# Attention features: the exponential's bias on GpSimd, the last two normalisations on VectorE

## The chip, the cores and the metric

The kernel runs on one core of a Trainium2 chip. A core has five engines, each with its own in-order queue of instructions: TensorE (PE, with the weight loads shown apart as PEld), VectorE (DVE), ScalarE (ACT), GpSimd (POOL) and SyncE (SP), which here only issues DMAs. They wait for each other through semaphores. The metric is the device time of one execution in microseconds; three runs of the kernel before gave 2180.44 (the median), 2174.37 and 2181.72.

## The reference, cut to what matters

Three layers follow each other. The first is linear attention with random features on 4 batches of 8 heads, 576 rows of 64 each; then comes a mixture of 8 experts whose gate is balanced by eight rounds of scaling; then a layer of width 2048. The change is in the first one:

```
def phi(x):
    proj = np.einsum('bhsd,md->bhsm', x, omega)
    sq = np.sum(x * x, axis=-1, keepdims=True) / 2.0
    h = proj - sq
    h = h - np.max(h, axis=-1, keepdims=True)
    return np.exp(h) / np.sqrt(m)
q_p, k_p = (phi(q_s), phi(k_s))
kv = np.einsum('bhsm,bhsd->bhmd', k_p, v)
z = np.sum(k_p, axis=2)
num = np.einsum('bhsm,bhmd->bhsd', q_p, kv)
den = np.einsum('bhsm,bhm->bhs', q_p, z)[..., None] + 1e-06
return (num / den)
```

## The kernel before

Attention is cut into 16 units (4 batches of 4 pairs of heads) and each unit into five chunks of rows, 128 and four times 112. A loop (L548) runs 20 iterations of five rounds r = 0 to 4. In iteration i, round r computes the features of chunk r of unit i, and a written plan (PLAN, L541) adds the later steps of the units before: `qkT` (transposes of the next unit's q and k), `kv` and `zT` (sums over the keys of unit i-1), `qpT` (transposes of unit i-2's normalised query features) and `num` (the numerator of unit i-3). The order of the work is this loop's order; no scheduler changes it.

The features of one chunk (`feat`, L387) go through a chain of engines. TensorE writes the projections of q and k for two heads, `pr`, into one PSUM bank (L393). VectorE takes the maximum over the features, `mx` (L403), and makes the bias of the exponential in two small subtractions on 4 numbers a row: `nm` = squares minus maximum (L405) and `nb` = `nm` minus squares (L407). ScalarE then runs four exponentials (L412), which write `ek` and `eq`; they are issued first in the next round. The bank of `pr` is free once these four are done.

The 7 rotating PSUM banks are shared by `pr`, the transposes `tr` and `qt`, `kv` and the numerator `nd`. In the steady loop the transpose `qt` of round 3 takes the bank that `pr` of round 1 had, `pr` of round 3 the one of round 0, and `nd` of round 4 the one of round 2; so the built program lets each of them wait for the exponentials of that chunk.

GpSimd does four kinds of work in this loop. It squares q and k of the next unit (`tmp`, L357, one of 128x640 elements in each of the rounds 0 and 1), it scales their sums (`sq`, L361, 128x10, in rounds 2 and 4), it multiplies `eq` of unit i-2 by the reciprocal of the denominators (L478: three products of 256 columns in round 0, two in round 1), and once in an iteration, from the sixth on, it takes a step of the weights' preparation. The denominators come from VectorE: per chunk and head a product with a sum (`jk`, L465), ten in an iteration, and a reciprocal (L475) after the first six and after the last four.

The main loop takes these in the order: `tmp` before the round's flush; then `mx`; then, as the flush works off its list, the sums with their products; and after the first of the list's items the generator steps on to `nm`, then to `nb`. The last two units' sums stand in iterations 16 and 17, where no features are left.

Of the kernel before, what the change touches and what calls it, by code (L numbers as in the profile page):

```python
# [13 lines left out]
ALU = mybir.AluOpType  # L14
# [5 lines left out]
def performer_moe_kernel(ctx, tc, q, k, v, omega, wg, w1, w2, win64, wout64, out):  # L20
    nc = tc.nc
    B, H, S, D = q.shape
    M = omega.shape[0]
# [233 lines left out]
    with ExitStack() as actx, tc.manual_schedule():  # L257
        pp = actx.enter_context(tc.tile_pool(name="pp", bufs=7, space=PSUM))

        def bank(name):  # L260
            return pp.tile([P, 512], F32, tag="b", name=name)
# [10 lines left out]
        NUN = B * NP  # L272
# [114 lines left out]
        def feat(u, c):  # L387

            qk, sq = T["qk", u], T["sq", u]
            o, n = CH[c]  # L390
            ps = bank(f"pr{u}_{c}")
            for i in range(2):
                nc.tensor.matmul(  # L393
                    ps[:n, 2 * M * i : 2 * M * (i + 1)], qk[:, i, o : o + n], bd, start=True, stop=True
                )
            mx = a2.tile([P, 4], F32, tag="mx", name=f"mx{u}_{c}", bufs=4)
            nm = a2.tile([P, 4], F32, tag="nm", name=f"nm{u}_{c}", bufs=4)
            nb = a2.tile([P, 4], F32, tag="nb", name=f"nb{u}_{c}", bufs=4)
            ps4 = ps.rearrange("p (i m) -> p i m", i=4)
            eq = a2.tile([P, 2, M], F32, tag="eq", name=f"eq{u}_{c}", bufs=16)  # L400
            ek = a2.tile([P, 2, M], F32, tag="ek", name=f"ek{u}_{c}", bufs=7)
            T["eq", u, c], T["ek", u, c] = eq, ek
            nc.vector.tensor_reduce(mx[:n], ps4[:n], AX.X, ALU.max)  # L403
            yield
            nc.vector.tensor_tensor(nm[:n], sq[:n, c], mx[:n], ALU.subtract)  # L405
            yield
            nc.vector.tensor_tensor(nb[:n], nm[:n], sq[:n, c], ALU.subtract)  # L407

            def exps():
                for i in (2, 3, 0, 1):  # L410
                    dst = (eq, ek)[i // 2][:n, i % 2]
                    nc.scalar.activation(dst, ps4[:n, i], AF.Exp, bias=nb[:n, i : i + 1])  # L412

            later.insert(0, exps)
            yield
# [34 lines left out]
        def zT(u):  # L450

            ps = pp.tile([P, 512], F32, tag="z", name=f"z{u}", bufs=1)
            zr = T.pop(("zr", u))
            for h in range(2):
                nc.tensor.transpose(
                    ps[:, h * M : (h + 1) * M], zr[:, h].rearrange("p t d -> p (t d)"), ident
                )
            dn = den[u % 2]

            def sums(cs):  # L460
                for c in cs:
                    n = CH[c][1]
                    for h in range(2):
                        junk = a2.tile([P, M], F32, tag="junk", name=f"jk{u}_{c}_{h}", bufs=2)
                        nc.vector.tensor_tensor_reduce(  # L465
                            junk[:n],
                            T["eq", u, c][:n, h],
                            ps[:n, h * M : (h + 1) * M],
                            1.0,
                            1e-6,  # L470
                            ALU.mult,
                            ALU.add,
                            dn[:n, c, h],
                        )
                nc.vector.reciprocal(dn[:, cs[0] : cs[-1] + 1], dn[:, cs[0] : cs[-1] + 1])  # L475
                for c in cs:
                    eq, n = T["eq", u, c], CH[c][1]
                    nc.gpsimd.tensor_tensor(eq[:n], eq[:n], dn[:n, c].to_broadcast([n, 2, M]), ALU.mult)  # L478

            def first():  # L480
                sums([0, 1, 2])
                laterv.append((2, lambda: sums([3, 4])))

            laterv.append((2, first))
# [63 lines left out]
        for i in range(NUN + 4):  # L548
            for r, items in enumerate(PLAN):
                if r in NORM and i + 1 < NUN:  # L550
                    norms(i + 1, NORM.index(r))
                if r in RED and T.get("red"):
                    laterv.append((3, T["red"].pop(0)))
                flush(feat(i, r) if i < NUN else iter(()))
                for fn, off, arg in items:
                    if 0 <= i + off < NUN:
                        fn(i + off, *(() if arg is None else (arg,)))
                if r == 0:
                    load(i + 2, 0, 1)
                if r == 3:  # L560
                    load(i + 2, 2)
                if i > 4 and r == SPL:
                    next(wprep, None)
                if i > 2 * NP + 4 and r in (1, 3):
                    next(xprep, None)
# [462 lines left out]
```

## Time and profile before

| What | Value |
|---|---|
| Median of three runs | 2180.44 us |
| The profiled execution | 2176.08 us |
| Its span, first to last instruction | 2174.3 us |
| PE, PEld, DVE busy | 98%, 87%, 84% of the span |
| ACT, POOL busy | 48%, 64% |
| Mean granted TensorE clock | 0.994 of full |

Busy shares are of the whole span, and the attention stage is only its first 212 us. Matmuls are pipelined and their ends modelled, so 98% of PE is not PE at its peak. In a timeline a row is one instruction or a merged run of equal ones: its start, its length, the engine, the line, what it writes and reads, and in brackets how long its engine sat idle before it and what the profile takes for the cause. Where an instruction waits for several semaphores, the cause named can be one that had long been done.

### The profile page before, as it was taken

To read this page: it belongs to the slowest core of one execution; us is meant where nothing else is said; L and a number is where in the kernel's file an instruction comes from. 1 tells how busy PE (TensorE), PEld (TensorE's weight loads), DVE (VectorE), ACT (ScalarE), POOL (GpSimd) and SP (SyncE) were. 2 spreads that over 40 slices of the span, in tenths; PEclk is the share of its full clock that TensorE was granted. 3 is DMA by queue.
4 is the path that set the end of the run, shared out by engine and by line. 5 is a ranking of instruction groups with operands and counts; after the bars stand their busy time and mean duration, and the time that the engine had idled before them with its cause. 6 is when DMAs were issued, how large, how long until landed. Compare 5 with 4: busy or idle time off the path is not lost.

```text
span 2174.3 us, 33292 instructions
## 1 busy us (share of the span) xinstructions
PE 2126.5 (98%) x10800; PEld 1891.3 (87%) x10800; DVE 1834.6 (84%) x3459; ACT 1048.6 (48%) x2577; POOL 1398.6 (64%) x1631
## 2 busy tenths in 40 slices
PE   8998999999999999999999999999999999999998
PEld 6786689989899899899999899899999989989997
DVE  8887588889898788798889778788886689999997
ACT  6676333333333433333333443333333377878775
POOL 5554677676767767676766767676766535656654
PEclk9999999999999999999999999999999999999999
DMA  4442413222323222232322233332222231222221
GB/s 114 130 105 87 146 68 121 78 96 83 97 81 100 91 95 88 95 100 80 103 82 91 74 107 99 102 99 82 97 79 80 69 102 44 88 88 73 73 76 37
DMA packets 184382, 195.71 MB, mean 90 GB/s; under 512 B 53392, under 2 KB 142992, under 8 KB 184208
## 3 DMA queue, kind: packets, MB, share of 16 engines
q1 hardware_dynamic: 177200, 184.09, 26.6%
q10 hardware_dynamic: 7008, 9.51, 1.2%
q8 instruction: 85, 1.39, 0.3%
q14 instruction: 89, 0.73, 0.1%
HBM read 171.00 MB, written 22.54 MB: 89 GB/s over the span
## 4 chain that ended last, share of the span: by engine, by line
PE 68%; DVE 14%; issue 4%; ACT 4%; DMA 1%; POOL 0%; DVEq 0%; SPq 0%; ACTq 0%; POOLq 0%
PE l L836 35%; PE b L727 13%; PE e L727 9%; PE a L727 9%; DVE t L819 3%; DVE t L820 2%; DVE t L812 2%; DVE acc L860 2%; DVE v L83 1%; ACT v L82 1%; PE p L801 1%; ACT t L818 1%; DVE x L83 1%; ACT u L82 1%; DVE acc L858 1%
## 5 line engine op out<-in xcount | busy, mean ns | idle before, releaser
L836 PE MATMUL l<-v,h 128*128 128x512 f32 x4320 | 1052.4, 393 | 8.0 <-ACT h L824 3.7
L836 PEld LDWEIGHTS l<-v,h 128*128 128x128 f32 x4320 | 806.8, 188 | 167.4 <-ACT h L824 4.4
L83 POOL TENSOR_TENSOR v<-rs,v 128x512 fp32r<-128x512 f32 x216 | 290.7, 1350 | 331.2 <-PE l L836 179.4
L866 DVE SCALAR_TENSOR_TENSOR acc<-l,pt,acc 128x512 f32<-128x512 f32 x540 | 397.6, 744 | 123.1 <-PE l L836 119.3
L83 POOL TENSOR_TENSOR u<-s,u 128x256 fp32r<-128x256 f32 x384 | 298.3, 788 | 114.6 <-ACT u L82 88.2
L727 PE MATMUL b<-x,u 128*128 128x384 f32 x1728 | 351.9, 338 | 3.0 <-DVE t L762 2.2
L727 PEld LDWEIGHTS b<-x,u 128*128 128x128 f32 x1728 | 309.1, 188 | 19.3 <-DVE t L762 2.6
L82 ACT CAST u<-s 128x256 fp32r<-128x256 f32 x384 | 154.4, 405 | 260.3 <-POOL s L162 233.3
L83 POOL TENSOR_TENSOR u<-rq,u 128x256 fp32r<-128x256 f32 x288 | 227.9, 791 | 21.4 <-ACT u L82 20.2
L727 PE MATMUL a<-x,u 128*128 128x384 f32 x1152 | 233.7, 337 | 0.6 <-ACT xo L520 0.6
L727 PE MATMUL e<-x,u 128*128 128x384 f32 x1152 | 233.1, 337 | 0.0
L801 PE MATMUL p<-x,u 128*128 128x384 f32 x1152 | 214.2, 340 | 0.8 <-ACT u L82 0.7
L727 PEld LDWEIGHTS a<-x,u 128*128 128x128 f32 x1152 | 205.5, 188 | 9.0 <-ACT xo L520 1.0
L801 PEld LDWEIGHTS p<-x,u 128*128 128x128 f32 x1152 | 204.7, 190 | 6.4 <-POOL u L83 1.6
L727 PEld LDWEIGHTS e<-x,u 128*128 128x128 f32 x1152 | 203.9, 189 | 1.2 <-DVE h L741 0.6
L825 POOL TENSOR_TENSOR h<-t,h 128x384 fp32r<-128x384 f32 x96 | 105.2, 1096 | 153.0 <-ACT h L824 148.4
L738 ACT ACTIVATE h<-b 128x384 fp32r<-128x384 f32 x96 | 47.2, 491 | 256.1 <-DVE b L776 252.4
L82 ACT CAST v<-rs 128x512 fp32r<-128x512 f32 x240 | 146.7, 621 | 35.0 <-PE l L836 34.1
L738 ACT ACTIVATE h<-t 128x384 fp32r<-128x384 f32 x96 | 50.4, 525 | 231.7 <-DVE t L763 231.7
L82 ACT CAST u<-rq 128x256 fp32r<-128x256 f32 x288 | 117.3, 407 | 1.6 <-ACT xo L880 1.6
L83 POOL TENSOR_TENSOR u<-rqi,u 128x256 fp32r<-128x256 f32 x96 | 93.0, 989 | 38.9 <-ACT u L82 36.5
L750 ACT COPY t<-a 128x384 f32<-128x384 f32 x96 | 46.1, 480 | 101.8 <-PE a L727 99.5
(140 smaller groups left out, 3120.3 us busy)
## 6 DMA issues: line engine op xcount, KB each, us to landing
rq<-in_moe_w_dram SPq DMA_DIRECT2D x96, 512.0 KB, 3.8
rs<-in_moe_w_dram SPq DMA_DIRECT2D x192, 256.0 KB, 2.7
rqi<-win SPq DMA_DIRECT2D x24, 512.0 KB, 4.8
rs<-wout SPq DMA_DIRECT2D x48, 256.0 KB, 2.8
xt<-xd SPq DMA_DIRECT2D x24, 384.0 KB, 5.5
r<-in_moe_w_in_dram SPq DMA_DIRECT2D x32, 256.0 KB, 3.2
r<-in_moe_w_out_dram SPq DMA_DIRECT2D x32, 256.0 KB, 3.0
xd<-xo SPq DMA_DIRECT2D x32, 144.0 KB, 1.8
```

Source lines behind the costliest of these rows:

```text
L82: nc.scalar.copy(dst[:, 0], src)
L83: eng.tensor_tensor(dst[:, 1], src, dst[:, 0].bitcast(F32), ALU.subtract)
L727: nc.tensor.matmul(ps[:, :TB], u[:, wi, c], x[:, xi, c], start=(start and m == 0), stop=(stop and m == 5), skip_group_check=True,)
L738: nc.scalar.activation(h[:, 0], src, AF.Relu)
L750: nc.scalar.copy(s1, A)
L801: nc.tensor.matmul(ps, u1[f + i][:, wi, c], ux[state["x0"] + 2 * t + i][:, xi, c], start=(m == 0), stop=(m == 11))
L812: nc.vector.tensor_tensor(s, u, ps, ALU.mult)
L819: nc.vector.scalar_tensor_tensor(s, gb, B1, s, ALU.add, ALU.mult)
L820: nc.vector.scalar_tensor_tensor(s, ga, A1, s, ALU.add, ALU.mult)
L825: nc.gpsimd.tensor_tensor(lo, s, hi.bitcast(F32), ALU.subtract)
L836: nc.tensor.matmul(ps, hh[f][:, hi, t : t + P], u2[n + f][:, wi], start=(f == 0 and i == 0), stop=(f == len(hh) - 1 and i == 2),)
L866: V.scalar_tensor_tensor(a, ps, p[:, e : e + 1], a, ALU.mult, ALU.add)
```

## The change

`nm` and `nb` are issued on GpSimd instead of VectorE, for all 16 units and five chunks: 160 small instructions. The product of `eq` with the reciprocal is issued on VectorE for units 14 and 15 (`u >= NUN - 2`), ten instructions, and stays on GpSimd for the others.

```diff
-            nc.vector.tensor_tensor(nm[:n], sq[:n, c], mx[:n], ALU.subtract)
+            nc.gpsimd.tensor_tensor(nm[:n], sq[:n, c], mx[:n], ALU.subtract)
             yield
-            nc.vector.tensor_tensor(nb[:n], nm[:n], sq[:n, c], ALU.subtract)
+            nc.gpsimd.tensor_tensor(nb[:n], nm[:n], sq[:n, c], ALU.subtract)
...
                 for c in cs:
                     eq, n = T["eq", u, c], CH[c][1]
-                    nc.gpsimd.tensor_tensor(eq[:n], eq[:n], dn[:n, c].to_broadcast([n, 2, M]), ALU.mult)
+                    eng = nc.vector if u >= NUN - 2 else nc.gpsimd
+                    eng.tensor_tensor(eq[:n], eq[:n], dn[:n, c].to_broadcast([n, 2, M]), ALU.mult)
```

GpSimd's queue in rounds 0 and 1 of iteration 4 stood before as follows; a name holds the unit and, after it, the chunk (`eq2_3` is chunk 3 of unit 2):

```order
L357 TENSOR_TENSOR tmp5_0_760<-qn1_99 128x640
L478 TENSOR_TENSOR eq2_0_423<-eq2_0_423,den0_108 128x256
L478 TENSOR_TENSOR eq2_1_466<-eq2_1_466,den0_108 112x256
L478 TENSOR_TENSOR eq2_2_504<-eq2_2_504,den0_108 112x256
L357 TENSOR_TENSOR tmp5_1_809<-kn1_101 128x640
L478 TENSOR_TENSOR eq2_3_533<-eq2_3_533,den0_108 112x256
L478 TENSOR_TENSOR eq2_4_560<-eq2_4_560,den0_108 112x256
```

The same place of GpSimd's queue now:

```order
L357 TENSOR_TENSOR tmp5_0_760<-qn1_99 128x640
L479 TENSOR_TENSOR eq2_0_423<-eq2_0_423,den0_108 128x256
L479 TENSOR_TENSOR eq2_1_466<-eq2_1_466,den0_108 112x256
L479 TENSOR_TENSOR eq2_2_504<-eq2_2_504,den0_108 112x256
L405 TENSOR_TENSOR nm4_0_766<-sq4_580,mx4_0_765 128x4
L407 TENSOR_TENSOR nb4_0_767<-nm4_0_766,sq4_580 128x4
L357 TENSOR_TENSOR tmp5_1_809<-kn1_101 128x640
L479 TENSOR_TENSOR eq2_3_533<-eq2_3_533,den0_108 112x256
L479 TENSOR_TENSOR eq2_4_560<-eq2_4_560,den0_108 112x256
L405 TENSOR_TENSOR nm4_1_815<-sq4_580,mx4_1_814 112x4
L407 TENSOR_TENSOR nb4_1_816<-nm4_1_815,sq4_580 112x4
```

The bias of chunk 0 stands behind three products and that of chunk 1 behind all five and the second `tmp`; on VectorE each stood right behind the reciprocal that the products wait for.

VectorE's queue at the end of the last unit, in iteration 17, now:

```order
L475 RECIPROCAL den1_109<-den1_109 128x6
L479 TENSOR_TENSOR eq15_0_2813<-eq15_0_2813,den1_109 128x256
L479 TENSOR_TENSOR eq15_1_2851<-eq15_1_2851,den1_109 112x256
L479 TENSOR_TENSOR eq15_2_2884<-eq15_2_2884,den1_109 112x256
L465 ISA jk15_3_0_3065,den1_109<-eq15_3_2905,z15_3033 112x128
L465 ISA den1_109 112x1
```

Before, the sums of chunk 3 (`jk15_3_0`) followed the reciprocal at once and the three products ran on GpSimd; now they stand between the two.

## Rows read from the trace of the kernel before

**Rows 1.** Windows: busy time by engine (x instructions), clock, DMA share, GB/s.
```profile
0.00:212.00 212.00, 189.47 (x1127) 154.32 (x1128) 176.25 (x695) 143.40 (x463) 108.75 (x170) 0.98 0.41 106
```
**Rows 2.** Timeline of the weight loads, one steady iteration of attention.
```profile
117.48 0.41 PEld L345 LDWEIGHTS qt<-ident,eq 128*128 128x128 f32 x4 [0.70 <-POOL eq L478]
...
119.17 0.78 PEld L509 LDWEIGHTS nd<-qp,kz 128*128 128x128 f32 x4 [0.56 <-ACT eq L412]
...
129.13 0.41 PEld L345 LDWEIGHTS qt<-ident,eq 128*128 128x128 f32 x4 [0.70 <-POOL eq L478]
```
**Rows 3.** Timeline of ACT ahead of the second of these waits.
```profile
127.92 0.62 ACT L412 ACTIVATE ek<-pr,nb 112x128 f32<-112x128 f32 x2 [1.78 <-PE pr L393]
128.44 0.62 ACT L412 ACTIVATE eq<-pr,nb 112x128 f32<-112x128 f32 x2
128.94 0.57 ACT L376 ACTIVATE qk<-tr 128x464 f32<-128x464 f32 x1
```
**Rows 4.** Timeline of DVE, rounds 0 and 1 of the same iteration.
```profile
121.94 0.69 DVE L403 TENSOR_REDUCE mx<-pr 128x4 f32<-128x512 f32 x1 [1.11 <-PE pr L393]
...
123.91 0.19 DVE L475 RECIPROCAL den<-den 128x6 f32<-128x6 f32 x1
124.02 0.12 DVE L405 TENSOR_TENSOR nm<-sq,mx 128x4 f32<-128x4 f32 x1
...
125.97 1.29 DVE L405 TENSOR_TENSOR nm<-sq,mx 112x4 f32<-112x4 f32 x1
127.36 0.47 DVE L407 TENSOR_TENSOR nb<-nm,sq 112x4 f32<-112x4 f32 x1
```
**Rows 5.** Timeline of POOL over the same rounds.
```profile
124.25 1.78 POOL L478 TENSOR_TENSOR eq<-eq,den 128x256 f32<-128x256 f32 x3 [0.59 <-DVE nm L405]
126.00 1.25 POOL L357 TENSOR_TENSOR tmp<-kn 128x640 f32<-128x640 f32 x1
127.20 1.18 POOL L478 TENSOR_TENSOR eq<-eq,den 112x256 f32<-112x256 f32 x2
```
**Rows 6.** Timeline of POOL, a small instruction and what follows it.
```profile
85.31 0.24 POOL L361 TENSOR_SCALAR sq<-sq 128x10 f32<-128x10 f32 x1 [2.78 <-DVE nm L405]
85.63 0.73 POOL L164 TENSOR_TENSOR s<-rq 128x256 f32<-128x256 f32 x1
```
**Rows 7.** Timeline of POOL: round 0's products, first, an uneven, last two iterations.
```profile
29.19 1.21 POOL L478 TENSOR_TENSOR eq<-eq,den 128x256 f32<-128x256 f32 x2 [0.90 <-DVE nm L405]
...
78.10 1.75 POOL L478 TENSOR_TENSOR eq<-eq,den 128x256 f32<-128x256 f32 x3
...
172.54 1.75 POOL L478 TENSOR_TENSOR eq<-eq,den 128x256 f32<-128x256 f32 x3 [0.17 <-DVE nm L405]
...
185.00 1.78 POOL L478 TENSOR_TENSOR eq<-eq,den 128x256 f32<-128x256 f32 x3 [2.51 <-DVE nm L405]
```
**Rows 8.** Timeline of PE in the iteration of 78.10.
```profile
81.69 0.37 PE L345 MATMUL qt<-ident,eq 112*128 112x112 f32 x1 [1.47 <-POOL eq L478]
```
**Rows 9.** Windows behind that wait and in a late iteration with idle PE.
```profile
82.00:85.00 3.00, 3.00 (x8) 2.15 (x7) 2.18 (x8) 3.00 (x11) 0.45 (x2) 0.50 0.28 78
...
177.00:180.00 3.00, 1.60 (x9) 1.11 (x9) 2.90 (x11) 2.08 (x8) 0.68 (x2) 1.00 0.00 0
```
**Rows 10.** Timeline of several engines, iteration 15 and the end of unit 15.
```profile
187.67 0.63 ACT L412 ACTIVATE ek<-pr,nb 112x128 f32<-112x128 f32 x2 [1.04 <-PE pr L393]
...
201.40 0.19 DVE L475 RECIPROCAL den<-den 128x6 f32<-128x6 f32 x1
...
201.76 3.61 POOL L478 TENSOR_TENSOR eq<-eq,den 128x256 f32<-128x256 f32 x5 [2.94 <-DVE den L465]
...
202.44 0.18 DVE L475 RECIPROCAL den<-den 128x4 f32<-128x4 f32 x1
...
204.85 0.45 PE L345 MATMUL qt<-ident,eq 112*128 112x112 f32 x1 [0.26 <-POOL eq L478]
```
**Rows 11.** Lines of DVE in the attention stage: an elementwise product on SBUF.
```profile
L224 DVE TENSOR_TENSOR xt<-xt 128x768 f32<-128x768 f32 x3 | 2.9, 952 | 0.0
```

## The prediction

> **What bounds the kernel now.** I read the windows first, then the loop's timeline engine by engine, backwards from where TensorE waits. The attention stage is the first 212 us, and only it is touched; in it PE is busy 189 us, DVE 176, ACT 143 and POOL 109 [rows 1]. No engine is full by these shares, and POOL, which gets the work, has the most room; so the question is not who has time but which wait closes the loop.
>
> In the steady part one iteration repeats every 11.65 us: the transpose `qt` of round 3 starts at 117.48 and again at 129.13 [rows 2]. Both times PE has waited 0.70 us, and the row names POOL's product `eq`. That had ended: its last run starts at 127.20 and takes 1.18, so 128.38 [rows 5]. What ended last is on ACT: the exponentials of chunk 1 run from 127.92 to 128.44 + 0.62 = 129.06, and `qt` starts 0.07 us later [rows 3]. It takes the PSUM bank of that chunk's `pr`. The exponentials in turn had waited 1.78 us; the row names PE, but they start 0.09 us after `nb` of chunk 1 ended on DVE, at 127.36 + 0.47 = 127.83 [rows 3, 4]. So the loop is: `qt`, the matmuls behind it, `mx` of round 0, the six sums, the reciprocal at 123.91, the second half on DVE, `nb` of chunk 1, the exponentials, the bank, `qt`. DVE is on this path from 121.94, where it had waited 1.11 us for PE [rows 4], to 127.83. In the same way `nd` of round 4 waits 0.56 us for the exponentials of chunk 2 [rows 2].
>
> **What the change does to this loop.** On DVE `nm` and `nb` of chunk 1 stood right behind the second reciprocal. On POOL they stand behind three products, the pair of chunk 0, `tmp` and two products, in a queue that starts after the first reciprocal. Three terms:
>
> Taken away on DVE: `nm` of chunk 1 takes 1.29 us against 0.12 for that of chunk 0, and `nb` 0.47 [rows 4]. The long one runs beside POOL's `tmp`, 126.00 to 127.25 [rows 5]. Without it DVE would be through about 1.5 us earlier in each iteration.
>
> The Trainium skill ("SBUF — State Buffer", section "Who interferes with whom") says that a VectorE instruction with two SBUF inputs is blocked by a GpSimd instruction that reads SBUF until that one ends. The trace agrees: 1.29 us beside a `tmp` of 1.25. By that rule alone the change takes a blocked instruction away and the kernel gets faster; this is a rival below.
>
> Added on POOL: POOL can start the first product at 124.25, as before, since reciprocal, sums, `mx` and PE ahead of it are unchanged. By the start-to-start distances the three products take 126.00 - 124.25 = 1.75, `tmp` 1.20, the two products 1.18 [rows 5]: 128.38 without the new instructions. Two pairs come on top, of chunk 0 and of chunk 1. The trace has no such pair on POOL. The nearest row is the scaling of 128x10 elements, 0.24 us, with 0.32 to the start of the next instruction [rows 6]; so a pair costs 0.48 to 0.64, and I take 0.50. From below, 0.24 (each as short as on DVE, 0.12 [rows 4]); from above, 1.18 (each like a product of 256 columns, 1.78 / 3 = 0.59 [rows 5]). With 0.50, `nb` of chunk 1 ends at 128.38 + 1.00 = 129.38, against 127.83: **1.55 us later** (1.03 to 2.91). The exponentials, `qt` and all behind it come that much later, in each turn of the loop. Nothing hides it: DVE's gained time lies ahead of `mx`es that now wait for the same late PE, and ACT and PE only wait.
>
> `nb` of chunk 0 also moves, from behind the first reciprocal to about 126.5, 2 us later. The exponentials of chunk 0 then hold up `pr` of round 3, which takes their bank. That wait stands ahead of `qt` on PE's queue and shorter than the delay of `qt`; it is contained in the 1.55 and not added. In rounds 2 to 4 the pairs follow work that POOL has done early; the exponentials there are queued behind those of chunk 1 on ACT, so I cost these pairs at nothing, with at most 3 x 0.50 in an iteration if ACT were not the later one.
>
> How many turns: round 0's products begin with 29.19 and end with 185.00, 14 times [rows 7]. Thirteen of them, to 172.54, have the `tmp` of the next unit: 13 x 1.55 = 20.2 us. In the uneven one at 78.10, POOL is the late engine already (PE waits 1.47 us for a product there [rows 8]); its chain, 78.10 + 1.75 + 0.50 + 1.20 + 1.18 + 0.50 = 83.2, and 1.2 for exponentials, lets `qt` start at 84.5, where now its last part starts at 81.69: 3 us instead of 1.55, so 1.5 more. The one at 185.00 has no `tmp`: 185.00 + 1.75 + 0.50, then 1.18 + 0.50, makes 188.93, and the exponentials start at 187.67 now, so about 0.09 after a `nb` of 187.58 [rows 10]: 1.35. Iterations 0 and 1 have no products; POOL's `tmp` blocks the pair on either engine, so 0, with 1 us to either side.
>
> **The second edit.** For units 14 and 15 nothing competes for DVE. Unit 15's first reciprocal ends at 201.59, POOL's products then take 3.61 us, and the transpose of chunk 3 starts at 204.85 [rows 10]. A product on DVE I put at 0.39 us, an estimate between 0.952 for 768 columns [rows 11] and 0.12 for 4 [rows 4]. Then 201.59 + 3 x 0.39, the sums and reciprocal of the second half (202.62 - 201.59 = 1.03 [rows 10]) and one product give 204.18: 0.67 gained, for two units 1.3. Bounds: nothing (blocked by POOL's own splits in the same stretch) and 2.5.
>
> **The sum.** 20.2 + 1.5 + 1.35 - 1.3 = +21.8 us. On the profiled execution, 2176.08: 2197.8. That execution is 4.4 below the median shown; the mean of it and the three runs is 2178.2, and I predict from that: **2200.0 us**. The later stages are bound by their own work and move back as a whole.
>
> **Rivals.**
> 1. The lock was the cost (faster). If the pair on POOL finished as early as a DVE free of blocking would have, PE could win back its waits, 0.70 + 0.56 = 1.26 us an iteration [rows 2], 13 x 1.26 + 1.3 = 17.7: 2160.5. For it: the 1.29 us row. Against: POOL is in order, and the row of products is now ahead of the pair. It decides if the pair ends before 127.83.
> 2. The delay is swallowed (no change). ACT idles 1.78 us ahead of these exponentials [rows 3], and the other banks could carry PE on. Against: that idle time is the wait for `nb` itself, and the bank follows within 0.07 us. It would leave only the tail's -1.3: 2177.
> 3. The clock falls too (slower still). PE's waits grow from 1.26 to 2.8 us an iteration. After the wait of rows 8 the granted clock was 0.50, that is 1.2 GHz, for at least 3 us [rows 9], which costs half of that, 1.5. In every turn this is 13 x 1.5 = 19.5 more: 2219.5. Against: a late stretch with PE busy for 1.60 of 3 us kept 1.00 [rows 9], and the new waits are split over `pr`, `qt` and `nd`. The page "TensorE: Matmul & The Clock Gate" of the Trainium skill, section "Part 1: The HAM clock gate", ties the clock to recent idleness; the two windows agree as far as they go.
>
> **How the numbers follow.** Forecast 0.78, rival 1 0.06, rival 2 0.06, rival 3 0.10. The forecast's own range, with a pair from 0.24 to about 0.9 and the tail's bounds, is 2190 to 2213. The range for 8 in 10 is 2188 to 2215, which takes in a clock that falls in some turns. A change of 0.3% (6.5 us) is what can be told from none here: slower 0.88, the same 0.06, faster 0.06.
>
> **What would show it.** The starts of round 0's products are 13.2 us apart instead of 11.65. On POOL `nm` and `nb` take about 0.25 each, behind the products; ACT's exponentials of chunk 1 start some 5.2 us after the first product instead of 3.7; PE's waits ahead of `pr` of round 3 and `qt` together grow by 1.55; DVE shows no `nm` of over 1 us and idles instead. The first matmuls of the next stage begin some 21 us later. If the products' starts stay 11.65 apart, the loop is not closed by these exponentials and I am wrong; if they come 14.7 or more apart with a clock below 1.00, rival 3 holds.

## The result: slower, by 0.66%

The changed kernel took 2192.11 us (median of five, 2188.38 to 2198.97) against 2180.44 for the kernel before (five runs, 2174.37 to 2181.91). The medians are 11.7 us apart, 0.54%. The ratio estimated from the runs is 1.0066, with an interval from 1.0054 to 1.0079, which is 12 to 17 us. The profiled execution took 2192.11 us; its span is 2190.3, against 2174.3 before.

The change lies in the attention stage, which ends 19.7 us later: the first weight load of the next stage starts at 230.68 instead of 210.96 (timelines of the weight loads, before and after).

```profile
210.96 1.01 PEld L727 LDWEIGHTS a<-x,u 128*128 128x128 f32 x6 [1.04 <-ACT xo L520]
```
```profile
230.68 0.99 PEld L728 LDWEIGHTS a<-x,u 128*128 128x128 f32 x6 [1.04 <-ACT xo L521]
```

What DVE gave away is seen in the windows over the stage (in the order of [rows 1]): DVE is busy for 142 us instead of 176, POOL for 132 instead of 109. PE is busy for 195 us instead of 189, but of 231 us instead of 212: its busy share falls from 89% to 84%.

```profile
0.00:231.00 231.00, 194.84 (x1123) 158.17 (x1124) 141.85 (x545) 143.49 (x463) 131.69 (x320) 0.97 0.37 97
```

The timeline of POOL in a steady iteration, over the rounds of [rows 5]:

```profile
125.77 1.76 POOL L479 TENSOR_TENSOR eq<-eq,den 128x256 f32<-128x256 f32 x3 [0.70 <-DVE den L475]
127.48 0.20 POOL L405 TENSOR_TENSOR nm<-sq,mx 128x4 f32<-128x4 f32 x1
127.76 0.20 POOL L407 TENSOR_TENSOR nb<-nm,sq 128x4 f32<-128x4 f32 x1
127.91 1.25 POOL L357 TENSOR_TENSOR tmp<-kn 128x640 f32<-128x640 f32 x1
129.12 1.18 POOL L479 TENSOR_TENSOR eq<-eq,den 112x256 f32<-112x256 f32 x2
130.26 0.20 POOL L405 TENSOR_TENSOR nm<-sq,mx 112x4 f32<-112x4 f32 x1
130.54 0.20 POOL L407 TENSOR_TENSOR nb<-nm,sq 112x4 f32<-112x4 f32 x1
...
138.64 1.76 POOL L479 TENSOR_TENSOR eq<-eq,den 128x256 f32<-128x256 f32 x3 [0.70 <-DVE den L475]
```

The products start 138.64 - 125.77 = 12.87 us apart instead of 11.65. A pair takes 127.91 - 127.48 = 0.43 us. The bias of chunk 1 ends at 130.74, 4.97 us after the first product; before it was 127.83 - 124.25 = 3.58. The timelines of ACT and of the weight loads (compare [rows 3] and [rows 2]) show who waits for it:

```profile
127.99 0.62 ACT L412 ACTIVATE ek<-pr,nb 128x128 f32<-128x128 f32 x2 [3.02 <-POOL nb L407]
...
130.78 0.63 ACT L412 ACTIVATE ek<-pr,nb 112x128 f32<-112x128 f32 x2 [1.14 <-POOL nb L407]
131.29 0.63 ACT L412 ACTIVATE eq<-pr,nb 112x128 f32<-112x128 f32 x2
```
```profile
129.19 0.70 PEld L393 LDWEIGHTS pr<-bd,qk 128*112 128x112 f32 x4 [0.94 <-ACT eq L412]
...
131.99 0.41 PEld L345 LDWEIGHTS qt<-ident,eq 128*128 128x128 f32 x4 [1.17 <-POOL nm L405]
...
133.45 0.78 PEld L510 LDWEIGHTS nd<-qp,kz 128*128 128x128 f32 x4 [0.33 <-ACT eq L412]
```

`pr` of round 3 now waits for the exponentials of chunk 0, `qt` for those of chunk 1 (they end at 131.92, `qt` starts 0.07 later; the row names `nm`, which was done at 130.46), `nd` for those of chunk 2. Together 2.44 us an iteration against 0.70 + 0.56 = 1.26 [rows 2]: 1.18 more, which is nearly the whole growth of the period, 1.22. DVE has no long `nm` any more and idles instead:

```profile
127.18 0.68 DVE L403 TENSOR_REDUCE mx<-pr 112x4 f32<-112x512 f32 x1
...
130.35 0.69 DVE L403 TENSOR_REDUCE mx<-pr 112x4 f32<-112x512 f32 x1 [1.76 <-PE pr L393]
```

In the uneven iteration (weight loads, then windows) `pr` waits 4.88 us, and in the 5 us behind it the granted clock is 0.55 of full, close to the lower of its two levels, 1.2 GHz:

```profile
89.03 1.30 PEld L393 LDWEIGHTS pr<-bd,qk 128*112 128x112 f32 x4 [4.88 <-ACT eq L412]
```
```profile
90.00:95.00 5.00, 5.00 (x16) 3.79 (x15) 1.28 (x4) 4.38 (x16) 1.55 (x8) 0.55 0.07 25
```

### The profile page after: what moved, and what is told of

It is laid out like the page before. It is cut to its first block, busy times and chain, and to the rows that moved or that the text cites. A ratio compares the mean times of both kernels' runs of the same rounds, so it can differ in the third digit from the quotient of the medians.

```text
span 2190.3 us, 33353 instructions
## 1 busy us (share of the span) xinstructions
PE 2130.7 (97%) x10800; PEld 1895.5 (87%) x10800; DVE 1796.4 (82%) x3309; ACT 1050.2 (48%) x2577; POOL 1421.5 (65%) x1781
## 3 DMA queue, kind: packets, MB, share of 16 engines
q8 instruction: 85, 1.39, 0.3%
## 4 chain that ended last, share of the span: by engine, by line
PE 81%; DVE 8%; issue 4%; POOL 3%; ACT 2%; DMA 2%; SPq 0%; DVEq 0%; POOLq 0%; ACTq 0%
PE l L837 41%; PE b L728 13%; PE a L728 9%; PE e L728 9%; PE p L802 6%; PE pr L393 1%; DVE t L820 1%; POOL eq L479 1%; POOL tmp L357 1%; DVE t L821 1%; DMA qn<-in_q_dram 1%; DVE t L813 1%; DVE x L83 1%; PE nd L510 1%; DVE acc L861 1%
## 5 line engine op out<-in xcount | busy, mean ns | idle before, releaser
L403 DVE TENSOR_REDUCE mx<-pr 112x4 f32<-112x512 f32 (+1 forms) x80 | 54.6, 683 | 74.1 <-PE pr L393 73.5
```

## The experiments

Each ratio is against the kernel before, run on the same chip. "Period" is the distance between the starts of round 0's products in a steady turn. Where a stretch of a profile is compared, it is one profile of each kernel. The question is what made the loop longer: the two instructions as such, the engine that they are on, or their place in GpSimd's queue; and whether the second edit bought anything.

**Only the first edit** (all products on GpSimd):

```diff
-                    eng = nc.vector if u >= NUN - 2 else nc.gpsimd
+                    eng = nc.gpsimd
```

> All 80 bias pairs on GpSimd, the products of units 14 and 15 left on GpSimd as before. Theory (the place in GpSimd's queue closes the loop): round 0's products start 12.88 us apart as in the changed kernel, against 11.65 before; the end of unit 15 looks like the kernel before, so it ends 0.5 to 1.5 us later than the changed kernel: ratio to before 1.007 to 1.008. Rival (each small GpSimd instruction costs, wherever it stands): the same time, so this run tells only the second edit's share.

2192.66 us, ratio 1.0060 (1.0046 to 1.0074), period 12.87. So the first edit is the whole loss. But the stage did not end later than in the changed kernel, as was expected: the next one starts at 229.83, 0.85 earlier. The total does not tell what the second edit is worth; the parts tell more. From the last iteration's first product (204.26 here, 206.17 in the changed kernel) to that start it is 25.57 us here and 24.51 there: by these two profiles the second edit gains 1.06 us. The 1.9 that this run was ahead by then is the difference between two executions of the same loop.

**Only the second edit** (the bias back on VectorE):

> Only the second edit: products of units 14 and 15 on VectorE, the bias stays on VectorE. By the prediction's step the attention stage ends 1.3 us earlier than in the kernel before, so the next stage's first matmul at 209.7 us, ratio 0.9994. By the other theory, taken from the changed kernel's trace (the last product took 0.93 us beside GpSimd's split instead of 0.42) and from the run without this edit, whose stage ended 0.85 us earlier than the changed kernel's, it gains nothing: first matmul at 211.0 to 212.0, ratio 1.0000 to 1.0005. The place of that matmul decides, since the times cannot tell these apart.

The next stage starts here:

```profile
209.92 1.01 PEld L728 LDWEIGHTS a<-x,u 128*128 128x128 f32 x6 [0.99 <-ACT xo L521]
```

1.04 us earlier than before, 0.75 of it behind the last iteration's first product (25.21 against 25.96 us). This speaks against the theory of no gain, and the prediction's 1.3 looks a little too much; but both rest on single profiles, and the same stretch differs by more between kernels that all have this edit (23.47 to 26.79 us). The time was 2172.60, ratio 0.9982 (0.9973 to 0.9991): clearly faster, and by more than this gain. In the two profiles the rest is behind attention, where the kernels are alike: from that load to the end it is 2170.2 - 209.92 = 1960.3 here and 2174.3 - 210.96 = 1963.3 before.

**Only the pair of chunk 1 on GpSimd**, second edit kept:

```diff
-            nc.gpsimd.tensor_tensor(nm[:n], sq[:n, c], mx[:n], ALU.subtract)
+            be = nc.gpsimd if c == 1 else nc.vector
+            be.tensor_tensor(nm[:n], sq[:n, c], mx[:n], ALU.subtract)
...
-            nc.gpsimd.tensor_tensor(nb[:n], nm[:n], sq[:n, c], ALU.subtract)
+            be.tensor_tensor(nb[:n], nm[:n], sq[:n, c], ALU.subtract)
```

> Only the pair of chunk 1 on GpSimd, second edit kept. If the loop is closed by the bias of chunk 1 behind all five products and the second tmp, that bias ends at 128.38 + 0.44 = 128.82 instead of 127.83: 0.99 later, period 12.4 to 12.65 us, ratio 1.0045 to 1.006. If the cost is mostly that of chunk 0's pair, whose exponentials hold the bank of pr in round 3 (0.94 us of wait there in the changed kernel), the period stays at or below 11.9 and the ratio at or below 1.0015.

2186.16 us, ratio 1.0042 (1.0030 to 1.0054), period 12.25: between the two forecasts, nearer to the first. The timelines of POOL and of the weight loads say why:

```profile
121.34 1.78 POOL L480 TENSOR_TENSOR eq<-eq,den 128x256 f32<-128x256 f32 x3 [0.47 <-DVE nm L406]
...
125.72 0.20 POOL L408 TENSOR_TENSOR nb<-nm,sq 112x4 f32<-112x4 f32 x1
```
```profile
127.17 0.41 PEld L345 LDWEIGHTS qt<-ident,eq 128*128 128x128 f32 x4 [1.71 <-POOL sq L361]
...
128.34 0.89 PEld L511 LDWEIGHTS nd<-qp,kz 128*128 128x128 f32 x4
```

The bias ends 125.92 - 121.34 = 4.58 us after the first product, 1.00 later than before, as computed, and `qt` waits 1.01 longer. But `nd` no longer waits at all, where it had 0.56: a wait that grows takes over a part of the next one on the same queue. So 1.01 - 0.56 = 0.45 is what the two waits add; the period grew by 0.60, and where the other 0.15 lies was not found.

**The pairs of chunks 2 to 4 on GpSimd**, those of 0 and 1 on VectorE (`c > 1` in the same place):

> The changed kernel, but only the pairs of chunks 2, 3 and 4 on GpSimd; those of chunks 0 and 1 on VectorE as before. Theory: the pair of chunk 1 is again right behind the second reciprocal, so the period stays 11.65 us and the ratio is 0.999 to 1.001, although 48 of 80 pairs have moved. Rival (cost by the instruction): three fifths of the loss, 1.004.

2178.26 us, ratio 0.9999 (0.9990 to 1.0008). The verdict is the first theory's, the period is not: 12.08 instead of 11.65, because `nd` waits 0.98 for chunk 2, whose pair stands behind GpSimd's scaling of `sq`, and that waits for VectorE's sum (weight loads; POOL one turn later):

```profile
123.23 0.78 PEld L511 LDWEIGHTS nd<-qp,kz 128*128 128x128 f32 x4 [0.98 <-ACT eq L413]
```
```profile
133.30 0.24 POOL L361 TENSOR_SCALAR sq<-sq 128x10 f32<-128x10 f32 x1 [0.86 <-DVE sq L360]
133.61 0.20 POOL L406 TENSOR_TENSOR nm<-sq,mx 112x4 f32<-112x4 f32 x1
```

The prediction had cost these pairs at nothing; alone they cost 0.43 us a turn. The next stage starts at 216.62, 5.7 us later than before. The total shows nothing of it: in the two profiles 2.6 us are made up behind attention (see below), and the other 3.1 are not seen in the ratio.

**All pairs on GpSimd, but ahead of the products:**

```diff
             nc.gpsimd.tensor_tensor(nm[:n], sq[:n, c], mx[:n], ALU.subtract)
-            yield
             nc.gpsimd.tensor_tensor(nb[:n], nm[:n], sq[:n, c], ALU.subtract)
...
+            def prods(cs):
...
+                laterv.append((2.5, lambda: prods([3, 4])))
...
             laterv.append((2, first))
+            laterv.append((2.5, lambda: prods([0, 1, 2])))
```

> The changed kernel with the pair issued ahead of the products in GpSimd's queue, tmp still ahead of the pair. Theory: the pair of chunk 1 waits for three products and tmp, not for the two products behind it: it ends at 127.20 + 0.44 = 127.64 in the clock of the kernel before, 0.2 us ahead of 127.83; period about 11.45 us, ratio 0.997 to 1.000. Rival (cost by the instruction, 80 pairs on GpSimd): 1.0066 as the changed kernel.

2178.72 us, ratio 1.0001 (0.9991 to 1.0010), period 11.82. The number of instructions on GpSimd is that of the changed kernel, and of the 1.22 us that a turn had lost 1.05 are back: what cost was the place. The next stage starts at 214.97, still 4.0 us later than before; that the total shows no loss is due to the stretch behind attention, 4.2 us shorter in this profile. The pair of chunk 1, still behind the second `tmp`, ends where it was expected, 118.74 - 115.34 = 3.40 us after the first product. The gain did not come all the same: `qt` waits a little less, 0.57 instead of 0.70, but `nd` waits 0.85 instead of 0.56 for chunk 2, whose pair now stands behind the two products and the scaling of `sq` (POOL, then weight loads):

```profile
117.05 1.25 POOL L357 TENSOR_TENSOR tmp<-kn 128x640 f32<-128x640 f32 x1
118.26 0.20 POOL L405 TENSOR_TENSOR nm<-sq,mx 112x4 f32<-112x4 f32 x1
118.54 0.20 POOL L406 TENSOR_TENSOR nb<-nm,sq 112x4 f32<-112x4 f32 x1
118.69 1.18 POOL L480 TENSOR_TENSOR eq<-eq,den 112x256 f32<-112x256 f32 x2
```
```profile
119.98 0.41 PEld L345 LDWEIGHTS qt<-ident,eq 128*128 128x128 f32 x4 [0.57 <-POOL eq L480]
...
121.96 0.78 PEld L513 LDWEIGHTS nd<-qp,kz 128*128 128x128 f32 x4 [0.85 <-ACT eq L411]
```

**The same, with `tmp` issued behind the round's flush, in rounds 1 and 2:**

```diff
-        NORM, RED, SPL = (0, 1), (2, 4), 4
+        NORM, RED, SPL = (1, 2), (3, 4), 4
...
-                if r in NORM and i + 1 < NUN:
-                    norms(i + 1, NORM.index(r))
...
                 flush(feat(i, r) if i < NUN else iter(()))
+                if r in NORM and i + 1 < NUN:
+                    norms(i + 1, NORM.index(r))
```

> As the last one, and the squares of the next unit (tmp) issued after the products of round 1 and after the features of round 2, their sums in rounds 3 and 4. Theory: the pair of chunk 1 ends at 126.00 + 0.44 = 126.44, 1.4 us ahead of the kernel before; TensorE gets back its waits of 0.70 and 0.56 us, the period falls to 10.4 to 10.7 us, ratio 0.991 to 0.995. Rival (cost by the instruction): 1.0066. Second rival (TensorE has another wait right behind): period above 11.3, ratio 0.998 to 1.000.

2167.86 us, ratio 0.9947 (0.9932 to 0.9961), period 11.33: faster than both kernels. The ratio is the first theory's, the period that of the second rival, another wait right behind: `qt` has no wait left; `nd` has, since chunk 2's pair now stands behind the first `tmp` (1.25 us):

```profile
103.73 0.78 PEld L513 LDWEIGHTS nd<-qp,kz 128*128 128x128 f32 x4 [0.76 <-ACT eq L411]
```

**Both `tmp` in rounds 2 and 3** (`NORM = (2, 3)`):

> Like the variant with the bias before the products and tmp behind the flush, but with the two tmp in rounds 2 and 3 instead of 1 and 2, so that the pair of chunk 2 stands ahead of both. If the position in GpSimd's queue is the whole cost, the 0.76 us wait of nd goes too: period 10.4 to 10.8 us, ratio 0.990 to 0.993 against the kernel before. If the late tmp and its sum on VectorE become the late ones instead (the squares for the next unit are then ready only in round 4), the period stays at 11.2 or above and the ratio at 0.994 or above.

2170.78 us, ratio 0.9974 (0.9965 to 0.9983). The loop does what the first theory says, 10.7 us, but the ratio does not. Over three turns PE is busy all of the time at the full clock (windows):

```profile
101.17:133.40 32.23, 32.23 (x212) 28.46 (x212) 23.77 (x97) 26.43 (x89) 25.09 (x61) 1.00 0.44 111
```

But the first product starts at 33.69 us, where it was 28.33 with `tmp` in rounds 1 and 2: in the first iterations the exponentials come late (weight loads), and the gain is eaten at the start.

```profile
21.09 0.30 PEld L423 LDWEIGHTS kv<-vn,ek 112*128 112x128 f32 x2 [1.96 <-ACT ek L411]
```

**Only the later `tmp`**, bias and products as in the kernel before:

> The kernel before with only tmp moved behind the flush of rounds 2 and 3; both edits undone, the bias on VectorE. If the place of tmp was all that the kernel before lacked, nm of chunk 1 is no longer blocked for 1.29 us, the period falls to 10.4 to 10.8 us and the ratio to 0.990 to 0.993, as good as with the bias on GpSimd. If the pair on VectorE is then blocked by the products (0.59 us each) and that of chunk 2 by tmp, the period is 11.0 to 11.6 us and the ratio 0.996 to 1.000, and the move of the bias to GpSimd is worth something once it is placed ahead.

2188.48 us, ratio 1.0054 (1.0041 to 1.0066), period 12.56: slower than either theory allowed. The timelines of DVE and POOL:

```profile
117.18 2.41 DVE L407 TENSOR_TENSOR nb<-nm,sq 112x4 f32<-112x4 f32 x1
```
```profile
117.18 1.19 POOL L478 TENSOR_TENSOR eq<-eq,den 112x256 f32<-112x256 f32 x2 [0.17 <-DVE nm L405]
118.32 1.26 POOL L357 TENSOR_TENSOR tmp<-qn 128x640 f32<-128x640 f32 x1
```

`nb` of chunk 1 starts with the first of two products and ends at 119.59, when the `tmp` behind them ends (119.58). That is 4.36 us after round 0's first product (115.23), where it was 3.58 before. In both places of `tmp` that were tried, the bias on VectorE was stopped by what GpSimd did at that moment; on GpSimd it is only queued, and that can be arranged. So the move of the bias is worth something once it stands ahead. Whether the bias on VectorE, with the products put later as in the runs above, would do as well was not tried.

**The last version**: `tmp` in rounds 1 and 2 in the first two iterations and in 2 and 3 from then on:

```diff
-                if r in NORM and i + 1 < NUN:
-                    norms(i + 1, NORM.index(r))
+                at = NORM if i > 1 else (1, 2)
+                if r in at and i + 1 < NUN:
+                    norms(i + 1, at.index(r))
```

> The bias on GpSimd ahead of the products, the two tmp behind the flush of rounds 1 and 2 in iterations 0 and 1 and of rounds 2 and 3 from then on. With both in rounds 2 and 3 throughout, PE was busy without a gap at a period of 10.7 to 10.8 us, but round 0's products began at 33.69 instead of 28.33 us. If those 5.4 us were lost only because the first two iterations waited for the later squares, the first matmul of the next stage falls from 205.8 to 200.4 to 201.5 us, ratio 0.992 to 0.9945 against the kernel before. If the start is regained but lost again in the uneven iteration, where a load decides, it stays at 204 to 206 us and the ratio at 0.996 to 0.9975.

2164.87 us (2158.43 to 2168.52), ratio 0.9936 (0.9919 to 0.9953), the lowest of all, though the interval overlaps that of 0.9947. It contains the second edit, which alone gave 0.9982. The first theory holds: the next stage starts at 200.58, 9.3 us earlier than with the second edit alone, and in the middle of the stage PE is busy for 39.9 of 40 us (weight load; windows).

```profile
200.58 1.01 PEld L732 LDWEIGHTS a<-x,u 128*128 128x128 f32 x6 [0.99 <-ACT xo L524]
```
```profile
110.00:150.00 40.00, 39.90 (x260) 34.98 (x259) 30.30 (x121) 32.07 (x108) 30.40 (x73) 1.00 0.41 107
```

## Why the prediction was right, step by step

The median was put at 2200.0 us, and 2192.11 lies inside the range. The profiled execution was put at 2197.8 and took 2192.11: 5.7 less, 2.0 of it in the attention stage and 3.7 behind it. The other 2.1 is that the forecast for the median was counted from a mean that lay above the profiled execution. The mechanism was right: the loop is closed by the bias of chunk 1, and GpSimd's queue makes it later. Two runs show it: the pair of chunk 1 alone on GpSimd brings nearly two thirds of the loss (1.0042 of 1.0066), and the reordered kernel, with as many instructions on GpSimd, has a period of 11.82 us instead of 12.87. The sizes, from the starts of round 0's products in the two profiles (29.19 and 30.32 for the first, 185.00 and 206.17 for the last) and the start of the next stage:

| Term | Predicted | Measured |
|---|---|---|
| Bias of chunk 1 later, in a steady turn | 1.55 | 4.97 - 3.58 = 1.39 |
| Period, in a steady turn | 1.55 | 1.22 (11.65 to 12.87) |
| Iterations 0 and 1, to the first product | 0 +- 1 | 1.13 |
| From the first to the last product, 13 turns | 20.2 + 1.5 = 21.7 | 20.04 |
| From the last product to the next stage | 1.35 - 1.3 = 0.05 | 24.51 - 25.96 = -1.45 |
| Behind attention, to the end of the span | 0 | 1959.6 - 1963.3 = -3.7 |
| Sum, on the profiled execution | 21.8 | 16.0 |

The period was put 0.33 us too long. Of this 0.14 is the pair, 0.43 us where 0.50 was taken, twice. The other 0.19 is that only the delay of `qt` was counted: `nd`'s wait fell from 0.56 to 0.33, since `qt` now stands longer ahead of it. The run with chunk 1 alone shows the same exchange in full, 0.56 to nothing.

The pairs of chunks 2 to 4, cost at nothing, are not free by themselves (0.43 in a turn, in the run with only these); in the changed kernel they are covered by the later chunk 1. The 1.13 us at the start lies just outside the bound and is not shown to be the change's: that start is at 28.44 with only the second edit, 0.75 ahead of the kernel before, and the two programs are alike up to there. It and the missing 1.5 at the end largely cancel, which is luck.

The uneven iteration was well sized by luck: the two turns around it (62.87 to 89.39 before, 68.80 to 99.99 after) grew by 4.67, predicted 2 x 1.55 + 1.5 = 4.6. But `pr` of round 3 waited there, 4.88 us for the exponentials of chunk 0, with a lower clock behind it, and not `qt`. The prediction's own sum, too, gives 84.4 - 81.69 = 2.7 us and not 3, and it sets the start of the whole `qt` against that of its last part.

The last turn's 1.35 is not in the end result: without the second edit this end took 25.57 us against 25.96 before. The delay itself came; in that run `kv` of unit 15 starts 1.17 us later after the first product (214.53 - 204.26 = 10.27 against 194.10 - 185.00 = 9.10). But the next waits of the weight loads, for the products of unit 14, shrank from 0.36 + 1.15 us to 0.32. This is again the exchange of one wait for another. The second edit was worth a little less than the 1.3 that was said, as far as single profiles show: 1.06 between the two kernels with the first edit, 0.75 between those without it. A product on VectorE took 0.42 us (predicted 0.39), but that of chunk 3 of unit 15, the first of the two in this row, took 0.93 beside GpSimd's conversion of `x`, as the bound "blocked by POOL's own splits" had it (DVE and POOL). The expectation of the run with the second edit alone calls it the last product; the last one took 0.41:

```profile
225.05 1.26 DVE L479 TENSOR_TENSOR eq<-eq,den 112x256 f32<-112x256 f32 x2
```
```profile
223.90 1.80 POOL L83 TENSOR_TENSOR x<-xt,x 128x768 fp32r<-128x768 f32 x1 [7.89 <-ACT x L82]
```

The 3.7 us behind attention were not foreseen, and their cause stays open. The time from the next stage's first load to the end differs from kernel to kernel in these profiles, from 1959.0 (chunk 1 alone) to 1964.0 us (only the later `tmp`), though the instructions there are the same. It falls into two groups: 1962.2 to 1964.0 in the three kernels without the second edit (the one before, the first edit alone, only the later `tmp`), 1959.0 to 1961.3 in the eight with it. So the second edit may have a part in it, and its ratio of 0.9982 fits; but there is one profile of each kernel, and the medians with and without it on top of the first edit (2192.11 and 2192.66) show no such gain. Between the kernel before and the changed one the difference is in the last matmuls `l`: from 1700 us on, PE's waits for `h` and `v` there are 3.7 and 2.8 us before, 1.1 and 2.2 after. These waits alone do not set the stretch: with both `tmp` in rounds 2 and 3 they are 3.7 and 2.8 as well, and it takes 1960.2.

Of the rivals, the first (the lock was the cost, faster) needed the pair to end before 127.83; it ended 1.39 later in the loop. But its idea holds where the pair is placed ahead and `tmp` behind it: PE then wins back the waits, and the last version is 0.64% faster, the second edit included. The second (delay swallowed) falls with the period. Of the third (the clock falls in every turn) only single iterations show something: the steady turns with waits of 0.94, 1.17 and 0.33 us kept a clock of 1.00, and behind the 4.88 it was 0.55.

## What to carry to other kernels

A small instruction costs its place in an in-order queue, not its duration: two instructions of 0.2 us, moved to an engine with half its time free, added 1.2 us to each turn, because 4 us of other work stood ahead of them. Before moving an instruction to a "free" engine, write down that engine's queue at the point where the result is wanted, and move what need not stand there (here the squares for the next unit) behind it in the same edit. And add up waits along the queue that sets the end, not one by one: when one grows, the next often shrinks.

## What the runs showed of the hardware

A VectorE subtraction of 4 numbers a row, 0.12 to 0.16 us when free, was held for 2.41 us by three GpSimd instructions in a row, two products and a `tmp`. The Trainium skill ("SBUF — State Buffer", section "Who interferes with whom") says that a VectorE instruction with two SBUF inputs contends with a GpSimd instruction that reads SBUF, and that the ports they share are an exclusive lock. The trace agrees that the VectorE instruction blocks; but here it did not get in after the first GpSimd instruction, and its hold ended with the third. The 1.29 us row of the prediction is a case of the same kind: that `nm` starts at 125.97, while the third product still runs (to 126.03), and is through only with the `tmp` behind it (127.26 and 127.25) [rows 4, 5]. In the same kernel `nb` got in between two products: it ended at 127.83, and the first of them ended about 127.79 (an estimate, half of the row of two) [rows 4, 5]. What decides between the two was not tried.

GpSimd's price for this tiny subtraction is 0.20 us, and a pair of dependent ones takes 0.43 from its start to that of the `tmp` behind it. The product of 256 columns takes 0.42 us on VectorE and 0.61 on GpSimd (medians in the changed kernel).
